# Attention with a gated MLP: the left keys of two heads in one whole product, and the gate's left tokens two blocks at a time

## The chip, the cores and the metric

The kernel runs on one core of one Trainium2 chip. The metric is the device time of the program in microseconds (us), as the median of several runs. The profile shows one execution of it; its span is the time from the first to the last instruction. TensorE is called PE here, VectorE DVE, ScalarE ACT, GpSimd POOL, and SyncE, which issues most transfers, SP.

## What is computed

Eight batches, 12 heads, 448 tokens, 64 features per head. Cut to what matters:

```python
def _attn_ref(q, k, v, g_q, g_k):
    q_n, k_n = (rmsnorm(q, g_q), rmsnorm(k, g_k))
    scores = scale * np.matmul(q_n, k_n.transpose(0, 1, 3, 2))
    scores = scores - np.max(scores, axis=-1, keepdims=True)
    attn = np.exp(scores)
    attn = attn / (np.sum(attn, axis=-1, keepdims=True) + 1e-09)
    return np.matmul(attn, v)

def _moe_ref(x, w_in, g_ln, w_sg, b_sg, w_out):      # x: (8, 448, 768), the heads side by side
    h = gelu_tanh(x @ w_in)                          # 1024 features
    u, v = (h[..., :512], h[..., 512:])
    v_n = layernorm(v) * g_ln
    v_s = np.einsum('ts,bsd->btd', w_sg, v_n) + b_sg[None, :, None]
    return x + (u * v_s) @ w_out
```

448 tokens are three tiles of 128 and one of 64. These last 64 are what the change is about: 64 left keys of each head in attention times v, and 64 left tokens in the gate, the product with w_sg.

## The kernel before

**Precision.** A product of two numbers of full precision is made of three products of halves: each operand is split into a high part and a low part (vh and vl, xh and xl, ws_h and ws_l), and high times high, high times low and low times high are summed in PSUM.

**Pairs and units.** Two heads make a pair, two pairs a unit; there are 48 pairs, six to a batch, and 24 units. A unit's 896 queries are seven tiles of 128. `scores` (L375) makes for each tile the products with the keys (L389) for both heads, the maximum (DVE, L392), the exponentials with their sums (ACT, L394), the high part (ACT, L397) and the low part (DVE, L398), and transposes them by DMA into `at_all` (L403). There a pair has 14 blocks of 128 keys: blocks 0 to 6 of the high parts and 7 to 13 of the low ones. In each seven, blocks 0 to 2 are keys of the first head, 4 to 6 keys of the second, and block 3 has 64 left keys of the first head in its lower partitions and 64 of the second in its upper ones. Two PSUM buffers of two banks each hold the scores (`ps_s`).

**PV.** `load_v` (L286) brings v for three pairs in four transfers, into a tile of seven blocks of 64 columns laid out in the same way. `vsquares` (L343) sums its squares for a scale, `vsplit` (L363) makes vh and vl from it (L369 on ACT, L370 on DVE). `pv` (L431) makes a pair's output in one PSUM bank, the first head in partitions 0 to 63 and the second in 64 to 127. Twelve steps of two matmuls each, one for a head: three steps with the left keys, 64 rows by 64 columns each, and nine with 128 rows by 64 columns. Ahead of them `recips` (L406) makes the row of reciprocals of the sums (POOL, PE at L423, ACT). Behind them the output is scaled and split into xh and xl (L450 to L454).

**The MLP.** `moe` (L477) works on one batch. The v half of h comes first (L510 for the three whole token tiles; L513 for the left 64 tokens, whose two halves of the features stand above each other in a bank), then the u half (L568), with the layer norm in between. Then the gate: for each of four feature blocks f, nine products over whole token tiles and three over the 64 left tokens, which use 64 rows of the array (rows 0 to 63 for f = 0 and 1, rows 64 to 127 for f = 2 and 3, L598); then bias (DVE, L603), the product with u (POOL, L604), the high part (ACT, L605) and the low parts (POOL, L607 and L608). Then the output projection with the residual (L632 to L648). All its PSUM tiles, and a few small ones, share three banks (`ps_m`).

**Order.** The functions are generators. The main loop (from L699) goes over the pairs. In each it merges the steps of three streams by the fraction of them that is done: the scores (8 or 6 steps for a pair), pv of the pair before (4 steps, `SV`) and moe of the batch before (11 steps for most pairs, `MR`). Each `yield` ends a step. The batch's moe starts one pair into the next batch and is spread over some five pairs; for the first and the last batch it starts before its batch is complete (`early`), and the last one has no attention beside it. The Tile framework gives every instruction a number in order of emission; its planner puts the instructions of each engine in order with a simulated timeline, the lowest number first among those that are ready. Instructions of moe go through `low` (L658): it adds an offset (200 or 100) to the number, and after each step sets the number back to what it was:

```python
p = tc.cur_priority
tc.cur_priority = max(1, p + off)
...
next(gen)
...
tc.cur_priority = p
```

So a step of moe does not move the numbers of what is emitted after it. At run time each engine takes its instructions in the planned order.

## Time and profile before

| | |
|---|---|
| median of three runs | 1035.32 us (1034.66 to 1037.95) |
| profiled execution | 1033.44 us |
| its span | 1031.6 us |
| mean granted clock of PE | 0.916 of full speed |
| busy: PE, DVE, ACT, POOL | 829.0, 733.3, 738.1, 386.9 us |
| matmuls | 5844 |

Busy time of PE is the union of its matmuls' times. Matmuls overlap in the pipeline, so what one costs is read from the starts of its neighbours. In a group, `128*64` is the form of the array that a matmul uses: rows by columns. Two matmuls that use different halves of the rows or the columns can run at the same time.

### The profile page before, as it was taken

The page shows a single profiled execution, that of the slowest core. Times are in us where ns is not written, and L with a number is a line of the kernel's source. Part 1 is how long each engine was busy: PE and PEld are TensorE (multiplying, and loading weights), DVE is VectorE, ACT ScalarE, POOL GpSimd, SP SyncE. Part 2 cuts the span into 40 slices and gives each one's busy share as a digit, 9 for nine tenths or more (in the row PEclk, how much of TensorE's full clock was granted, in tenths as well). Part 3 has the DMA queues.
Part 4 walks back from the last instruction along what each step waited for, and adds up shares of the span by engine and source line. Part 5 has one row for each costly group of instructions (what it writes and reads, how often), then busy time and mean ns, then how long its engine had stood idle before and what let it go on. Part 6 is the DMA issues. An engine that isn't in the chain of part 4 may idle for free.

```text
span 1031.6 us, 16639 instructions
## 1 busy us (share of the span) xinstructions
PE 829.0 (80%) x5844; PEld 421.1 (41%) x5844; DVE 733.3 (71%) x1332; ACT 738.1 (72%) x1449; POOL 386.9 (38%) x403
## 2 busy tenths in 40 slices
PE   0243666858798997899689998999779998998798
PEld 0111222324444563346234553446324563454246
DVE  6698888999587667786677758786669666766230
ACT  3767779877868767777768767987777776877351
POOL 1468614567253505243251606341533414030021
PEclk9976687969899999999699998999889999999899
DMA  6998748776886398478886488959967676556102
GB/s 163 214 228 191 166 115 196 185 176 130 181 197 150 88 204 180 98 170 145 186 175 147 99 194 183 182 123 176 194 142 160 141 166 125 106 135 123 40 1 62
DMA packets 448004, 155.70 MB, mean 151 GB/s; under 512 B 404336, under 2 KB 441776, under 8 KB 447920
## 3 DMA queue, kind: packets, MB, share of 16 engines
q1 hardware_dynamic: 447344, 154.18, 69.0%
q8 instruction: 46, 0.75, 0.3%
q10 hardware_dynamic: 576, 0.46, 0.2%
q14 instruction: 38, 0.31, 0.1%
HBM read 43.57 MB, written 11.01 MB: 53 GB/s over the span
## 4 chain that ended last, share of the span: by engine, by line
PE 34%; DVE 21%; ACT 19%; DMA 11%; issue 8%; SPq 4%; POOL 4%; ACTq 0%; POOLq 0%; DVEq 0%
PE pv L446 6%; ACT s L394 5%; DVE ahl L398 5%; PE s L389 4%; DVE nm L392 3%; ACT ahl L397 2%; DMA vr<-in_v_dram 2%; ACT sqk L308 2%; DMA raw<-in_moe_w_in_dram 2%; DMA at<-ahl 2%; POOL qk L330 2%; DMA qt<-hl 2%; DMA qk<-in_k_dram 2%; ACT hl L334 2%; SPq L336 1%
## 5 line engine op out<-in xcount | busy, mean ns | idle before, releaser
L394 ACT ACTIVATE s<-s,nm 128x448 f32<-128x448 f32 x336 | 204.0, 607 | 109.8 <-DVE nm L392 106.8
L398 DVE TENSOR_TENSOR ahl<-s,ahl 128x896 f16<-128x896 f32 x168 | 182.1, 1085 | 100.8 <-ACT ahl L397 99.8
L389 PE MATMUL s<-qt 64*128 64x448 f16 (+1 forms) x1152 | 143.2, 390 | 110.7 <-DVE ahl L398 76.4
L392 DVE TENSOR_REDUCE nm<-s 128x2 f32<-128x896 f32 x168 | 180.8, 1082 | 40.5 <-PE s L389 40.0
L397 ACT ACTIVATE ahl<-s 128x896 f16<-128x896 f32 x168 | 153.4, 920 | 5.3 <-DMA at<-ahl 3.1
L446 PE MATMUL pv<-at,vh 128*64 128x448 f16 (+1 forms) x768 | 122.7, 398 | 16.4 <-DMA at<-ahl 7.6
L413 POOL TENSOR_SCALAR rx<-sums 128x8 f32<-128x8 f32 x48 | 13.4, 278 | 311.8 <-ACT s L394 310.4
L389 PEld LDWEIGHTS <-qt 64*128 64x128 f16 (+1 forms) x1152 | 45.3, 102 | 177.2 <-issue 135.9
L330 POOL TENSOR_TENSOR qk<-qk,ny 128x896 f32<-128x896 f32 x46 | 80.8, 1774 | 85.8 <-DVE ny L125 82.3
L335 POOL TENSOR_TENSOR hl<-qk,hl 128x896 f16<-128x896 f32 x46 | 87.7, 1917 | 55.1 <-ACT hl L334 54.5
L568 PEld LDWEIGHTS <-wi 128*128 128x128 f16 x576 | 55.9, 100 | 60.2 <-issue 14.1
L446 PEld LDWEIGHTS <-vh 128*64 128x64 f16 (+1 forms) x768 | 43.4, 117 | 84.3 <-issue 70.2
L309 DVE TENSOR_REDUCE ss<-sqk 128x14 f32<-128x896 f32 x48 | 51.8, 1080 | 29.2 <-ACT sqk L308 28.9
L394 ACT ACTIVATION_READ_ACCUMULATOR s<-s,nm 128x1 f32 x336 | 67.7, 201 | 0.0
L329 POOL TENSOR_TENSOR qk<-qk,gg 128x896 f32<-128x896 f32 x23 | 48.0, 2085 | 43.2 <-ACT sqk L308 39.3
L423 PE MATMUL row<-ident_h,rh 128*64 128x128 f16 (+1 forms) x384 | 36.7, 240 | 31.7 <-POOL rh L415 24.0
L604 POOL TENSOR_TENSOR gt<-gt,u 128x448 f32<-128x448 f32 x32 | 38.5, 1206 | 60.1 <-DVE gt L603 55.9
L446 PE MATMUL pv<-at,vl 128*64 128x448 f16 (+1 forms) x384 | 60.4, 394 | 0.0
L334 ACT ACTIVATE hl<-qk 128x896 f16<-128x896 f32 x48 | 44.9, 947 | 15.9 <-POOL qk L330 8.4
L308 ACT ACTIVATE sqk<-qk 128x896 f32<-128x896 f32 x48 | 45.6, 951 | 8.2 <-DVE ss L309 4.4
L510 PEld LDWEIGHTS <-xh 128*128 128x128 f16 x288 | 27.0, 101 | 49.2 <-issue 21.9
L369 ACT ACTIVATE vh<-vr,v_s 128x448 f16<-128x448 f32 x48 | 31.9, 668 | 19.7 <-PE pv L446 19.6
(996 smaller groups left out, 1960.8 us busy)
## 6 DMA issues: line engine op xcount, KB each, us to landing
out_dram<-ot SPq DMA_DIRECT2D x56, 192.0 KB, 2.9
vr<-in_v_dram SPq DMA_DIRECT2D x32, 192.0 KB, 3.3
raw<-in_moe_w_in_dram SPq DMA_DIRECT2D x12, 512.0 KB, 5.7
qk<-in_q_dram SPq DMA_DIRECT2D x47, 128.0 KB, 2.8
qk<-in_k_dram SPq DMA_DIRECT2D x47, 128.0 KB, 2.8
vr<-in_v_dram SPq DMA_DIRECT2D x32, 144.0 KB, 3.3
qk<-in_q_dram SPq DMA_DIRECT2D x47, 96.0 KB, 2.6
qk<-in_k_dram SPq DMA_DIRECT2D x47, 96.0 KB, 2.6
```

The source lines that it names most:

```text
L308: A.activation(out=skv, in_=U[u]["qk"][:, x].rearrange("p h c d -> p (h c) d"), func=AF.Square)
L309: V.tensor_reduce(out=SS[u][:, x], in_=skv, axis=AX.X, op=ALU.add)
L330: E.tensor_tensor(out=qk, in0=qk, in1=r["rs"][:, x * SSW:(x + 1) * SSW].unsqueeze(2).broadcast_to([P, SSW, D]), op=ALU.mult)
L334: A.activation(out=h_, in_=r["qk"][:, x], func=AF.Copy)
L335: E.tensor_tensor(out=l_, in0=r["qk"][:, x], in1=h_, op=ALU.subtract)
L389: mm(out=ps[r_, h, 0:S], lhsT=qt[hs, qx, t * P + r_.start:t * P + r_.stop], rhs=qt[hs, kx, j * S:(j + 1) * S], start=(m == 0), stop=(m == 2))
L392: V.tensor_reduce(out=nm, in_=ps[:, :, 0:S], axis=AX.X, op=ALU.max, negate=True)
L394: A.activation(out=ps[:, h, 0:S], in_=ps[:, h, 0:S], func=AF.Exp, bias=nm[:, h:h + 1], accum_out=sums[:, t, h:h + 1])
L397: A.activation(out=ahl[:, 0], in_=ps[:, :, 0:S], func=AF.Copy)
L398: V.tensor_tensor(out=ahl[:, 1], in0=ps[:, :, 0:S], in1=ahl[:, 0], op=ALU.subtract)
L446: mm(out=ps[h * HP:(h + 1) * HP], lhsT=vx[ks, c], rhs=at_all[ks, n + c, o:o + S], start=(k_ == 0), stop=(k_ == len(blocks) - 1), skip_grou ...
L568: done = mm(out=ps[:, 0:S], lhsT=ww[:, g, f * P:(f + 1) * P], rhs=xx, start=(n == 0), stop=(n == 17))
```

## The change

- **v with zeros.** A v tile has eight blocks of 64 columns instead of seven. The left keys of the two heads get a block each, side by side: the first head's stand in the lower partitions of block 3, the second head's in the upper ones of block 4, and the other halves are zero. The tiles are two fixed ones, and POOL writes their zeros once at the start. `vsquares` and `vsplit` go over eight blocks.
- **One product for both heads.** Blocks 3 and 4 of vh or vl are one stationary operand of 128 by 128. The left keys take three whole matmuls instead of six of 64 by 64. The other 18 matmuls stay as they are, but in another order. 24 become 21.
- **A pair's output in one block.** The two yields inside pv go, and one comes after the evacuation; pv has three steps, and `SV` is 3.
- **The left tokens of the v half.** In all batches but the first and the last, moe no longer yields inside the 36 products of the 64 left tokens.
- **The gate two feature blocks at a time.** f = 0 and 2 and then f = 1 and 3: nine whole products of the one, a yield, nine of the other, a yield, then the three products over the left tokens of both in turn, one in rows 0 to 63 and one in rows 64 to 127, each into its own bank. Then the rest for both, and a yield. The gate has six yields instead of eight.

```diff
--- before.py
+++ after.py
@@ -32,7 +32,7 @@
 
 VC, UC = (3,), (0, 1)
 
-SC, SV = 7, 4
+SC, SV = 7, 3
 
 NS, NV, NM = 2, 1, 3
 NQK, NVR, RAWB = 2, 2, 3
@@ -282,6 +282,11 @@
         U[u] = dict(qk=qk)
 
     VR = {}
+    C8 = C7 + 1
+    vr_all = [ld.tile([P, GV, C8, D], F32, name=f"vr{n}", bufs=1) for n in range(NVR)]
+    for x in vr_all:
+        G.memset(x[hi, :, CM], 0.0)
+        G.memset(x[lo, :, C4], 0.0)
 
     def load_v(i):
 
@@ -290,10 +295,10 @@
         if i >= NI:
             return
         b, g = divmod(i, NP)
-        vr = ld.tile([P, GV, C7, D], F32, name="vr", bufs=NVR)
+        vr = vr_all[i // GV % NVR]
         vp = vr.rearrange("p g c d -> p g (c d)")
         src = v[b, 2 * g:2 * (g + GV)].rearrange("(g h) (p c) d -> h p g (c d)", h=2, c=C7)
-        for h, half, s0, c0, n in ((0, lo, 0, 0, C4), (0, hi, 0, C4, CM), (1, lo, C4, C4, CM), (1, hi, CM, 0, C4)):
+        for h, half, s0, c0, n in ((0, lo, 0, 0, C4), (0, hi, 0, C4, CM), (1, lo, C4 + 1, C4, CM), (1, hi, C4, 0, C4)):
             nc.sync.dma_start(out=vp[half, :, s0 * D:(s0 + n) * D], in_=src[h][:, :, c0 * D:(c0 + n) * D])
         for j in range(GV):
             VR[i + j] = vr[:, j].rearrange("p c d -> p (c d)")
@@ -347,7 +352,7 @@
         b, g = divmod(i, NP)
         if g == 0:
             VS["part", b] = sml.tile([P, NP // GV], F32, name="vpart", bufs=2)
-        n = GV * C7 * D
+        n = GV * C8 * D
         sk = prep.tile([P, n], BF16, name="sqv", tag="t4", bufs=HLB)
         x = VR[i]
         A.activation(out=sk, in_=bass.AP(tensor=x.tensor, offset=x.offset, ap=[list(x.ap[0]), [1, n]]), func=AF.Square,
@@ -363,7 +368,7 @@
     def vsplit(i):
         r = R.setdefault(i, {})
         sc = VS[i // NP]["sc"]
-        vh, vl = (att.tile([P, C7, D], F16, name="v" + c, bufs=NVH) for c in "hl")
+        vh, vl = (att.tile([P, C8, D], F16, name="v" + c, bufs=NVH) for c in "hl")
         vr = VR.pop(i)
         vf = vh.rearrange("p c d -> p (c d)")
         A.activation(out=vf, in_=vr, func=AF.Copy, scale=sc)
@@ -432,21 +437,18 @@
         r = R[i]
         vh, vl = r["vh"], r["vl"]
         o = i % NAT * S
-
-        steps = [[(slice(0, P), c + h * C4) if c < CM else (slice(h * HP, (h + 1) * HP), CM) for h in range(2)]
-                 for c in range(C4)]
-        blocks = [(vx, n, hx) for vx, n in ((vh, 0), (vl, 0), (vh, C7)) for hx in steps]
-
-        blocks = blocks[CM::C4] + [x for n, x in enumerate(blocks) if n % C4 != CM]
         row = recips(i)
         yield
         ps = ps_v.tile([P, 512], F32, name="pv")[:, 0:S]
-        for k_, (vx, n, hx) in enumerate(blocks):
-            for h, (ks, c) in enumerate(hx):
-                mm(out=ps[h * HP:(h + 1) * HP], lhsT=vx[ks, c], rhs=at_all[ks, n + c, o:o + S],
-                   start=(k_ == 0), stop=(k_ == len(blocks) - 1), skip_group_check=True)
-            if k_ in (4, 8):
-                yield
+        parts = ((vh, 0), (vl, 0), (vh, C7))
+        for k_, (vx, n) in enumerate(parts):
+            mm(out=ps, lhsT=vx[:, CM:CM + 2].rearrange("p c d -> p (c d)"), rhs=at_all[:, n + CM, o:o + S],
+               start=(k_ == 0), stop=False, skip_group_check=True)
+        for c in range(CM):
+            for vx, n in parts:
+                for h in range(2):
+                    mm(out=ps[h * HP:(h + 1) * HP], lhsT=vx[:, c + h * (C4 + 1)], rhs=at_all[:, n + c + h * C4, o:o + S],
+                       start=False, stop=(c == CM - 1 and n == C7), skip_group_check=True)
         V.tensor_tensor(out=ps, in0=ps, in1=row, op=ALU.mult)
         xh = xp.tile([P, S], F16, name="xh")
         xl = xp.tile([P, S], F16, name="xl")
@@ -454,6 +456,7 @@
         V.tensor_tensor(out=xl, in0=ps, in1=xh, op=ALU.subtract)
         XT[i] = (xh, xl)
         del R[i]
+        yield
 
 
     def cluster(acts, done):
@@ -517,7 +520,7 @@
                 psv[t] = vg[:, tiles[t][1]]
             if early and t == 1 and g == NP - 1:
                 cluster([gelu_v(i) for i in range(2)], done)
-            if st % 2 == 1:
+            if st % 2 == 1 and (early or t != CM or g == NP - 1):
                 yield
         cluster([gelu_v(t) for t in order if not early or t == CM or t > 1], done)
         for t in range(CK):
@@ -578,7 +581,7 @@
                  for f in range(FT)], done)
         yield
         gh = mlp.tile([P, FT, S], F32R, name="gh", tag="vggh")
-        gl = []
+        gl = {}
         vh, vl = V2["vh"], V2["vl"]
         half = slice(b % 2 * HP, (b % 2 + 1) * HP)
         if b % 2 == 0:
@@ -586,26 +589,29 @@
         else:
             gth, gtl, _ = GT[b - 1]
         bb = W["bb"]
-        for f in range(FT):
-            ps = ps_m.tile([P, 512], F32, name="ms_", tag="mm")
-            n = 0
-            for t in range(CK):
-                p0, p1, o = 0, P, t * DH + f * P
-                if t == CM:
-                    p0 = f // 2 * HP
-                    p1, o = p0 + HP, t * DH + f % 2 * P
-                for vx, wx in ((vh, ws_h), (vh, ws_l), (vl, ws_h)):
-                    mm(out=ps[:, 0:S], lhsT=vx[p0:p1, o:o + P], rhs=wx[p0:p1, t], start=(n == 0), stop=(n == 11))
-                    n += 1
-                if t == 1:
-                    yield
-            gt = mlp.tile([P, S], F32, name="gt", tag="gt", bufs=NOT)
-            V.scalar_tensor_tensor(out=gt, in0=ps[:, 0:S], scalar=W["gw"][:, f:f + 1], in1=bb, op0=ALU.mult, op1=ALU.add)
-            G.tensor_tensor(out=gt, in0=gt, in1=u[f], op=ALU.mult)
-            A.activation(out=gh[:, f], in_=gt, func=AF.Copy)
-            gl.append(mlp.tile([P, S], F32R, name="gl", tag="ug", bufs=5))
-            G.tensor_tensor(out=gl[f], in0=gt, in1=gh[:, f].bitcast(F32), op=ALU.subtract)
-            G.tensor_tensor(out=gtl[:, f, half], in0=gt[:, SM:S], in1=gh[:, f, SM:S].bitcast(F32), op=ALU.subtract)
+        for f0 in range(2):
+            psf = {f: ps_m.tile([P, 512], F32, name="ms_", tag="mm") for f in (f0, f0 + 2)}
+            for f, ps in psf.items():
+                n = 0
+                for t in range(CM):
+                    o = t * DH + f * P
+                    for vx, wx in ((vh, ws_h), (vh, ws_l), (vl, ws_h)):
+                        mm(out=ps[:, 0:S], lhsT=vx[:, o:o + P], rhs=wx[:, t], start=(n == 0), stop=False)
+                        n += 1
+                yield
+
+            for n, (vx, wx) in enumerate(((vh, ws_h), (vh, ws_l), (vl, ws_h))):
+                for f, ps in psf.items():
+                    p0, o = f // 2 * HP, CM * DH + f0 * P
+                    mm(out=ps[:, 0:S], lhsT=vx[p0:p0 + HP, o:o + P], rhs=wx[p0:p0 + HP, CM], start=False, stop=(n == 2))
+            for f, ps in psf.items():
+                gt = mlp.tile([P, S], F32, name="gt", tag="gt", bufs=NOT)
+                V.scalar_tensor_tensor(out=gt, in0=ps[:, 0:S], scalar=W["gw"][:, f:f + 1], in1=bb, op0=ALU.mult, op1=ALU.add)
+                G.tensor_tensor(out=gt, in0=gt, in1=u[f], op=ALU.mult)
+                A.activation(out=gh[:, f], in_=gt, func=AF.Copy)
+                gl[f] = mlp.tile([P, S], F32R, name="gl", tag="ug", bufs=5)
+                G.tensor_tensor(out=gl[f], in0=gt, in1=gh[:, f].bitcast(F32), op=ALU.subtract)
+                G.tensor_tensor(out=gtl[:, f, half], in0=gt[:, SM:S], in1=gh[:, f, SM:S].bitcast(F32), op=ALU.subtract)
             yield
         idn = VS[b]["idn"]
         om = [out[x].rearrange("(p c) e -> c p e", c=C7) for x in (b - b % 2, b)]
```

## The prediction

> **What bounds the kernel now.** I read the page's busy shares first, then the busy time by stretches, then the chain that ended last.
>
> ```profile
> PE 829.0 (80%) x5844; PEld 421.1 (41%) x5844; DVE 733.3 (71%) x1332; ACT 738.1 (72%) x1449; POOL 386.9 (38%) x403
> ```
>
> ```profile
> 0.00:227.00 227.00, 110.13 (x690) 46.21 (x691) 190.92 (x343) 162.40 (x316) 112.08 (x98) 0.79 0.79 183
> 227.00:896.00 669.00, 599.22 (x4342) 308.01 (x4341) 489.26 (x905) 506.03 (x1002) 251.41 (x270) 0.95 0.74 156
> ```
>
> ```profile
> PE 34%; DVE 21%; ACT 19%; DMA 11%; issue 8%; SPq 4%; POOL 4%; ACTq 0%; POOLq 0%; DVEq 0%
> PE pv L446 6%; ACT s L394 5%; DVE ahl L398 5%; PE s L389 4%; DVE nm L392 3%; ACT ahl L397 2%; DMA vr<-in_v_dram 2%; ACT sqk L308 2%; DMA raw<-in_moe_w_in_dram 2%; DMA at<-ahl 2%; POOL qk L330 2%; DMA qt<-hl 2%; DMA qk<-in_k_dram 2%; ACT hl L334 2%; SPq L336 1%
> ```
>
> The columns of the second fence are stretch, length, then busy us of PE, PEld, DVE, ACT, POOL, then the granted clock. For the first 227 us DVE is the fullest engine (190.9 of 227). From 227 to 896 us, two thirds of the run, PE is busy 599.2 of 669, that is 0.90, against 0.73 for DVE and 0.76 for ACT. So a microsecond taken off PE in this stretch is worth at most about 0.9, and DVE and ACT have a quarter of their time free to hide a little more work. The chain is shared out, though: PE has only 34% of it, and the products of pv (L446) are its largest line.
>
> **PV: what the zero padding is worth.** The timeline of one pair's output (start, us, matmuls):
>
> ```profile
> 547.71 0.54 PE L568 MATMUL mu__5949<-xh,wi 128*128 128x448 f16 x2
> 548.18 0.38 PE L446 MATMUL pv<-at,vh 64*64 64x448 f16 x2
> 548.39 0.35 PE L446 MATMUL pv<-at,vl 64*64 64x448 f16 x2
> 548.58 1.04 PE L446 MATMUL pv<-at,vh 64*64 64x448 f16 x8
> 549.45 0.73 PE L446 MATMUL pv<-at,vl 128*64 128x448 f16 x6
> 550.02 0.73 PE L446 MATMUL pv<-at,vh 128*64 128x448 f16 x6
> ```
>
> Six 128*64 matmuls start 549.45 to 550.02, 0.57 us: the two heads run side by side, 0.19 us for the two. The two 64*64 matmuls of the left keys also go side by side (548.39 to 548.58, 0.19). So a pair has 12 passes now, and with three whole 128*128 products and nine pairs of column halves it has 12 again. 24 matmuls become 21 and no pass is saved. What can be saved is changes of tile form. A pass of mu takes half of 0.38 us; the two ahead of pv took 0.47 (547.71 to 548.18), so the change of form costs about 0.1 us.
>
> *Entry.* A block that starts in 128*128 form pays none of it where a 128*128 product stands directly ahead. I count 19 of 48 blocks so, the first at 196.39 us, the last here:
>
> ```profile
> 938.58 0.38 PE L510 MATMUL mv__10576<-wi,xl 128*128 128x512 f16 x1
> 938.89 0.38 PE L446 MATMUL pv<-at,vh 64*64 64x448 f16 x2
> ```
>
> No block follows a 64*64 form directly, so nothing is lost: 19 x 0.1 = 1.9 us. The change inside the block stays (64*64 to 128*64 before, 128*128 to 128*64 after).
>
> *One block instead of three.* In 23 of the 48 blocks a score tile (L389) comes in between. The first and the last:
>
> ```profile
> 80.35 0.74 PE L389 MATMUL s<-qt 64*128 64x448 f16 x6
> 81.03 0.38 PE L446 MATMUL pv<-at,vh 128*64 128x448 f16 x1
> ...
> 956.17 0.95 PE L446 MATMUL pv<-at,vh 128*64 128x448 f16 x3
> 957.06 0.74 PE L389 MATMUL s<-qt 64*128 64x448 f16 x6
> 957.73 0.57 PE L446 MATMUL pv<-at,vh 128*64 128x448 f16 x3
> ```
>
> The score tile's three passes take 0.67 (957.06 to 957.73) instead of 0.57, and there is a second change on the way in: 0.2 us for a break, and where it splits the two heads, as behind an odd number (x3, x1), another 0.19. I take 0.28, so 6.4 us in all. With the yields at blocks 4 and 8 gone, the score steps that were emitted between them come behind the whole block. A tile emitted earlier that becomes ready in the middle still breaks in. The bounds are 0 and 6.4; I take two thirds, 4.3, since with the block in the middle of the merge half of the score steps still stand ahead of it.
>
> **Gate: left tokens side by side.** Each batch has 4 feature blocks of 9 whole passes and 3 half-row passes. Emitted as here, six of the latter would run as three twice per batch: 6 x 0.19 = 1.14 us, and 4 of 8 changes of form, 0.4 us: 1.5 us a batch, 12.3 us in all. Whether they are issued so is for the planner, which sorts by a number. `low` puts the number back after each step of moe, so two steps with nothing of the attention emitted between them carry the same numbers and are woven together. The trace shows it, in the last gate and in the left tokens of the v half:
>
> ```profile
> 1000.66 0.36 PE L598 MATMUL ms__11010<-ws_h,vh 64*128 64x448 f16 x1
> 1000.86 0.35 PE L598 MATMUL ms__11010<-ws_l,vh 64*128 64x448 f16 x1
> 1001.14 0.36 PE L598 MATMUL ms__11030<-ws_h,vh 128*128 128x448 f16 x1
> ...
> 1001.91 0.35 PE L598 MATMUL ms__11030<-ws_l,vh 128*128 128x448 f16 x1
> 1002.19 0.36 PE L598 MATMUL ms__11010<-ws_h,vl 64*128 64x448 f16 x1
> 1002.48 0.36 PE L598 MATMUL ms__11030<-ws_h,vl 128*128 128x448 f16 x1
> ```
>
> ```profile
> 518.90 0.30 PE L513 MATMUL mv__5575<-wi,xh 128*64 128x256 f16 x1
> 519.13 0.39 PE L510 MATMUL mv__5655<-wi,xh 128*128 128x512 f16 x1
> 519.45 0.30 PE L513 MATMUL mv__5575<-wi,xh 128*64 128x256 f16 x1
> ```
>
> The gate's leftover block is a step of its own after the steps of f and f+2. After the change v has 10 steps and u 14, so f, f+2 and the leftovers are steps 24 to 26, at 0.227, 0.318 and 0.409 of the batch's third pair (11 steps a pair); the score steps of that pair fall at 0.25 and 0.417. Nothing lies between 0.318 and 0.409: the leftovers of f have numbers among those of f+2's nine products, are ready as soon as f's own nine are done, and go first, alone. The second two fall at 0.5, 0.591 and 0.682, with a score step at 0.583 and none behind it, the same. Then the gate has the 24 passes and 4 changes per two blocks that it has now. I take 2 of the 16 couples as joined (batch 0 has another merge): 1.5 us of the 12.3.
>
> *The v half.* Without its two inner yields the 36 products of the left tokens are one step, but the steps of t = 0 that follow start 9 numbers in, after the first half of one score tile. The weaving of six shown above starts earlier and stays six: 0, between +5 and -5 us (three weavings more or fewer in each of six batches, 0.3 us each: two changes of form and one half-wide pass).
>
> *The end.* The last gate has no scores to fill it. POOL needs three instructions per feature block:
>
> ```profile
> L604 POOL TENSOR_TENSOR gt<-gt,u 128x448 f32<-128x448 f32 x32 | 38.5, 1206 | 60.1 <-DVE gt L603 55.9 <-ACT u L577 2.1 <-ACT s L394 2.0
> L607 POOL TENSOR_TENSOR gl<-gt,gh 128x448 fp32r<-128x448 f32 x32 | 36.8, 1150 | 7.9 <-ACT gh L605 7.8
> L608 POOL TENSOR_TENSOR gtl<-gt,gh 128x64 fp32r<-128x64 f32 x32 | 10.3, 322 | 0.0
> ```
>
> That is 2.7 us a block, more than the 2.3 us of its 12 passes. Two blocks that end together start POOL later and leave it two blocks to finish, and the out projection takes f = 1 second where it now comes third. I charge 0.7 us (0 to 2.7). Elsewhere scores cover this.
>
> **What is added.** The v tile grows from 7 to 8 blocks of 64:
>
> ```profile
> L369 ACT ACTIVATE vh<-vr,v_s 128x448 f16<-128x448 f32 x48 | 31.9, 668 | 19.7 <-PE pv L446 19.6
> L353 ACT ACTIVATE sqv<-vr 128x1344 bf16<-128x1344 f32 x16 | 21.2, 1322 | 10.8 <-DMA vr<-in_v_dram 8.5 <-DVE ss L309 2.3
> L370 DVE SCALAR_TENSOR_TENSOR vl<-vr,v_s,vh 128x448 f16<-128x448 f32 x48 | 36.6, 764 | 3.0 <-ACT vh L369 3.0
> ```
>
> In proportion ACT gets 48 x 0.095 + 16 x 0.189 = 7.6 us and DVE 48 x 0.109 = 5.2 us. Their shares of the chain, 19% and 21%, make 2.5 us of it exposed; the bounds are 0 (the idle quarter hides it) and 12.8. The four memsets on POOL come before its first real work, when it has nothing else, and the v loads move the same bytes through SP: 0.
>
> **Sum.** PE saves 1.9 + 4.3 + 1.5 = 7.7 us, at 0.9 worth 6.9; less 2.5 and 0.7 leaves 3.7. The profiled execution took 1033.44 us (span 1031.6 and 1.84 around it), so 1029.7; the median of the runs is 1.88 above the profiled one, so 1031.6, and I say 1031.5. A difference of 0.3% (3.1 us) is about what can be told from no change.
>
> **Rivals.**
> *The left tokens do go side by side* (chance 0.15). The other 10.8 us x 0.9 = 9.7 come on top: about 1022. For it: couples of row halves do run together in the scores (957.06 above, six in 0.67). Against it: the woven rows.
>
> *No difference* (0.25). PE is 34% of the chain, not 90%: then the 7.7 us are worth 2.6 and the added 2.5 and 0.7 cancel it, about 1036. This also stands for "the change does not do what it says".
>
> *Slower: the unbroken block starves the softmax* (0.22). A score tile that now slips in waits up to the rest of the block, about 1.1 us (half of 12 passes), and with it DVE's maximum, ACT's exponentials and the two score buffers.
>
> ```profile
> PE s L389 <- DVE ahl L398: 76.4, 35, 9.0
> ```
>
> PE already idles 76.4 us ahead of scores for DVE to give a buffer back. In 23 blocks 1.1 us more is 25 us of delay; DVE and ACT hold 40% of the chain, so 10 us, less the 3.7: about 1041.6. It decides from 0.4 us per block on (23 x 0.4 x 0.4 = 3.7).
>
> *Slower by the clock* (0.05). Where PE is starved its granted clock falls: 0.79 in the first 227 us, 0.95 later. If longer waits give two more drops of 6.8 us at half speed, each costs 3.4: 1031.5 + 6.8 = 1038.3. [...]
>
> **Chances and range.** My sum 0.33, the gate 0.15, no difference 0.25, starved 0.22, clock 0.05. Faster 0.48, same 0.25, slower 0.27. Between 1022 and 1042 lie the rivals' times; less than 2 in 10 is outside, in the planner's reordering of everything else. My sum's own range is 1027 to 1032.
>
> **What would show it.** pv in 21 matmuls and about 2.5 us per unbroken block; fewer score tiles inside (8 or so of 48); single 64*128 rows of L598 still 0.19 apart with 128*128 rows between. L369 near 0.76 us, L370 near 0.87. I am wrong if the half-row products come two at a time, if idle time of L389 behind DVE grows past 85 us, or if the clock from 227 to 896 us leaves 0.95.

## The result: slower by 1.4%

The changed kernel took 1050.84 us (median of 4 runs, 1046.84 to 1055.37), the kernel before 1036.3 in the same comparison (1034.66 to 1037.95): a ratio of 1.0142, 95% interval 1.0093 to 1.019. I had said 1031.5, and 1022 to 1042. The profiled execution took 1049.1 us, 15.7 more than the one of before. The head of its page, the first line with the span, the next with each engine's busy time:

```profile
span 1047.3 us, 16365 instructions
...
PE 823.9 (79%) x5700; PEld 420.3 (40%) x5700; DVE 731.5 (70%) x1332; ACT 747.8 (71%) x1449; POOL 385.8 (37%) x407
```

PE is busy 5.1 us less (823.9 for 829.0), in 144 matmuls fewer, and the span is 15.7 us longer. So PE stands idle 223.4 us (1047.3 - 823.9) where it stood idle 202.6 (1031.6 - 829.0). The busy time by stretches (columns as in the prediction) says where:

```profile
0.00:227.00 227.00, 108.75 (x692) 46.08 (x692) 184.31 (x334) 163.21 (x315) 107.83 (x100) 0.80 0.74 175
227.00:896.00 669.00, 579.90 (x4079) 297.83 (x4080) 479.87 (x876) 501.94 (x977) 254.84 (x269) 0.92 0.72 156
```

In the first 227 us PE loses nothing: 692 matmuls for 690, though the kernel now has fewer to do. DVE, the fullest engine there, gets through 334 instructions for 343. Between 227 and 896 us PE is busy 579.9 us for 599.2, its granted clock falls from 0.95 to 0.92, and it gets through 4079 matmuls for 4342; about 93 of these 263 are products that the change merges (144 x 669 / 1032). DVE and ACT do less in the same time as well (876 instructions for 905, 977 for 1002). All three engines wait more. None has become the full one.

The clock has to be taken out of the busy times before they are compared. A block of pv where the clock is low, and two where it is not, from the timeline of the changed kernel (start, us, matmuls):

```profile
563.40 0.35 PE L599 MATMUL ms__6050<-ws_l,vh 128*128 128x448 f16 x1
563.70 0.35 PE L445 MATMUL pv<-at,vh 128*128 128x448 f16 x1
563.89 0.35 PE L445 MATMUL pv<-at,vl 128*128 128x448 f16 x1
564.08 0.35 PE L445 MATMUL pv<-at,vh 128*128 128x448 f16 x1
564.36 0.38 PE L450 MATMUL pv<-at,vh 128*64 128x448 f16 x2
...
566.18 0.36 PE L599 MATMUL ms__6050<-ws_h,vl 128*128 128x448 f16 x1
...
665.03 0.35 PE L571 MATMUL mu__7262<-xh,wi 128*128 128x448 f16 x1
665.22 0.35 PE L445 MATMUL pv<-at,vh 128*128 128x448 f16 x1
...
738.49 0.53 PE L445 MATMUL pv<-at,vh 128*128 128x448 f16 x1 [2.61 <-ACT sqv L358]
738.81 0.58 PE L445 MATMUL pv<-at,vl 128*128 128x448 f16 x1
739.18 0.58 PE L445 MATMUL pv<-at,vh 128*128 128x448 f16 x1
...
743.20 0.59 PE L132 MATMUL psc<-vpart,ones 128*128 128x2 f32 x2
```

The block at 563.70 lasts 2.48 us to the next start; the one at 738.49, behind 2.61 us of idle time, lasts 4.71, with passes 0.37 apart instead of 0.19. The granted clock in the trace is 0.5 or 1 in every record of the two kernels; the block at 738.49 lies in a half-clock stretch of 13.7 us that begins at 730.72, the one at 563.70 at full clock. So I add up the spans by three terms: PE's busy time with the half-clock part counted half ("work"), what the half clock cost, and idle time. Before: 768.8 + 60.2 + 202.6 = 1031.6. After: 753.9 + 70.0 + 223.4 = 1047.3. Work fell by 14.9 us, idle time rose by 20.8, the clock took another 9.8. The work is to be read with care: one of the experiments below changes no matmul and has 9.1 less of it. Busy time counts the modelled end of each run of matmuls, which may be why; that isn't shown.

The places of the idle time, from the groups of the page, first before, then after (behind the bars: busy us and mean ns, then idle time of PE just ahead of the group and its main releasers):

```profile
L389 PE MATMUL s<-qt 64*128 64x448 f16 (+1 forms) x1152 | 143.2, 390 | 110.7 <-DVE ahl L398 76.4
L446 PE MATMUL pv<-at,vh 128*64 128x448 f16 (+1 forms) x768 | 122.7, 398 | 16.4 <-DMA at<-ahl 7.6
```

```profile
L394 PE MATMUL s<-qt 64*128 64x448 f16 (+1 forms) x1152 | 138.6, 381 | 111.6 <-DVE ahl L403 78.2
L445 PE MATMUL pv<-at,vh 128*128 128x448 f16 x96 | 39.0, 406 | 30.1 <-DMA at<-ahl 9.4 <-ACT ahl L402 8.0 <-ACT row L431 7.1
```

Ahead of the scores the sums over the whole span are alike, 110.7 and 111.6, but two changes cancel in them. The wait for DVE alone, between 227 and 896 us, first before, then after (who waits for whom: us in total, times, longest):

```profile
PE s L389 <- DVE ahl L398: 21.0, 21, 3.0
PE s L394 <- DVE ahl L403: 32.5, 22, 4.8
```

In the first 227 us this wait fell from 55.2 to 45.6 us; where the time is lost it rose by 11.5. Ahead of pv PE waits 30.1 us instead of 16.4 over the span. Of these 13.7 us more, 6.9 fall between 227 and 896 us (12.4 for 5.5) and 6.4 in the first 227 us, where PE loses nothing. Ahead of the gate's products it waits 11.2 us in the stretch instead of 0.8, and ahead of the row of reciprocals 10.1 instead of 18.0. So PE's loss is spread over scores, gate and pv.

On the other side of pv stand the engines that evacuate it. Their waits before and after, over the whole span:

```profile
DVE pv L450 <- PE pv L446: 22.0, 11, 7.7
ACT xh L453 <- DVE pv L450: 18.4, 10, 6.2
```

```profile
PE s L394 <- DVE ahl L403: 78.2, 35, 11.0
DVE pv L452 <- PE pv L450: 36.1, 22, 8.5
ACT xh L455 <- DVE pv L452: 25.1, 15, 8.7
DVE nm L397 <- PE s L394: 23.7, 26, 2.2
```

DVE and ACT wait 61.2 us for a pair's output (36.1 + 25.1), before it was 40.4. In three of DVE's waits (up to 416.83, 743.31 and 971.78 us) the next split of a score tile had its input from ACT 0.4 to 0.7 us before the wait ended and ran only behind the scaling of pv; in the others its input came later. Whether PE's longer wait ahead of the scores comes from such waits, no run shows. DVE's own wait for scores fell (23.7; it was 40.0 before).

### The profile page after: what moved, and what is told of

Read it like the earlier page. It is cut to its first block, busy times and chain, and to the rows that moved or that the text cites. A ratio compares the mean times of both kernels' runs of the same rounds, so it can differ in the third digit from the quotient of the medians.

```text
span 1047.3 us, 16365 instructions
## 1 busy us (share of the span) xinstructions
PE 823.9 (79%) x5700; PEld 420.3 (40%) x5700; DVE 731.5 (70%) x1332; ACT 747.8 (71%) x1449; POOL 385.8 (37%) x407
## 4 chain that ended last, share of the span: by engine, by line
PE 35%; ACT 22%; DVE 20%; DMA 9%; issue 7%; POOL 4%; SPq 3%; ACTq 0%; POOLq 0%; DVEq 0%
ACT s L399 7%; PE pv L450 5%; DVE nm L397 5%; ACT ahl L402 4%; DVE ahl L403 4%; PE s L394 3%; DMA vr<-in_v_dram 2%; PE pv L445 2%; DMA raw<-in_moe_w_in_dram 2%; DVE vl L375 2%; DMA at<-ahl 2%; SPq L278 1%; DVE ss L314 1%; ACT sqv L358 1%; ACT vg L499 1%
## 5 line engine op out<-in xcount | busy, mean ns | idle before, releaser
L394 PE MATMUL s<-qt 64*128 64x448 f16 (+1 forms) x1152 | 138.6, 381 | 111.6 <-DVE ahl L403 78.2
L397 DVE TENSOR_REDUCE nm<-s 128x2 f32<-128x896 f32 x168 | 180.5, 1081 | 24.0 <-PE s L394 23.7
L418 POOL TENSOR_SCALAR rx<-sums 128x8 f32<-128x8 f32 x48 | 12.3, 256 | 277.1 <-ACT s L399 275.5
L450 PE MATMUL pv<-at,vh 128*64 128x448 f16 x576 | 102.7, 411 | 0.0
L445 PE MATMUL pv<-at,vh 128*128 128x448 f16 x96 | 39.0, 406 | 30.1 <-DMA at<-ahl 9.4
L450 PE MATMUL pv<-at,vl 128*64 128x448 f16 x288 | 59.3, 409 | 0.0
L374 ACT ACTIVATE vh<-vr,v_s 128x512 f16<-128x512 f32 x48 | 34.4, 721 | 34.3 <-PE pv L450 31.6
L450 PEld LDWEIGHTS <-vh 128*64 128x64 f16 x576 | 36.9, 125 | 48.0 <-issue 34.5
L452 DVE TENSOR_TENSOR pv<-pv,row 128x448 f32<-128x448 f32 x48 | 30.1, 627 | 36.1 <-PE pv L450 36.1
```

The source lines that it names most:

```text
L394: mm(out=ps[r_, h, 0:S], lhsT=qt[hs, qx, t * P + r_.start:t * P + r_.stop], rhs=qt[hs, kx, j * S:(j + 1) * S], start=(m == 0), stop=(m == 2))
L397: V.tensor_reduce(out=nm, in_=ps[:, :, 0:S], axis=AX.X, op=ALU.max, negate=True)
L445: mm(out=ps, lhsT=vx[:, CM:CM + 2].rearrange("p c d -> p (c d)"), rhs=at_all[:, n + CM, o:o + S], start=(k_ == 0), stop=False, skip_group_ ...
L450: mm(out=ps[h * HP:(h + 1) * HP], lhsT=vx[:, c + h * (C4 + 1)], rhs=at_all[:, n + c + h * C4, o:o + S], start=False, stop=(c == CM - 1 and ...
```

## The experiments

Three questions were open: which part of the change costs, whether it costs by its instructions or by the order in which the planner now puts all the others, and whether PE's work is worth anything. The theories are numbered alike in all expectations: 1 the unbroken block of pv, 2 the padded v (its tiles' dependencies or its wider instructions), 3 the gate's two open banks, 4 the order alone, 5 the block in any order, 6 the one step of the v half. All ratios are to the kernel before, run on the same chip, with their 95% intervals.

### One part undone

**Old steps of pv** in the changed kernel (padding, gate and v half kept):

```diff
+                if k_ in (2, 6):
+                    yield
+                k_ += 1
...
         del R[i]
-        yield
```

> The changed kernel with pv's products in three steps again, broken after the same number of passes as before, and SV = 4; the zero-padded v, the gate and the v half stay changed. Theory 1 (the unbroken block is the cost: PE waits for its inputs, 30 us idle ahead of pv instead of 16, and score tiles wait behind it): about 1037 to 1040, ratio to the kernel before 1.00 to 1.005, PE's idle time ahead of pv back to about 16 us. Theory 2 (the wider v tile on ACT and DVE): still 1.012 or more. Theory 3 (the gate's two open banks): still 1.012 or more. Theory 4 (no part costs by itself, the planner lays everything out anew and the order is worse by chance): anything between 0.99 and 1.015.

1.0137 (1.0108 to 1.0166). Undoing the block gives nothing back, where theory 1 allowed 1.005 at most. Its profile has 31.9 us of idle time ahead of pv, so this isn't tied to the block either.

**Old gate** in the changed kernel (diff of the change's gate, reversed):

> The changed kernel with the gate of before, one feature block after the other. Theory 3 (the gate's two open banks and the joint evacuation are the cost): 1.000 to 1.006, PE idle ahead of the gate's products back from 11 us to 1. Theories 1 and 2: still 1.012 or more, since the gate's left tokens ran singly in the changed kernel anyway. Theory 4: anything between 0.99 and 1.015.

1.0114 (1.0092 to 1.0135). Theory 3 allowed 1.006 at most, with PE's wait ahead of the gate back at 1 us; it is still some 8 us.

**Old steps of the v half** in the changed kernel:

```diff
-            if st % 2 == 1 and (early or t != CM or g == NP - 1):
+            if st % 2 == 1:
```

> The changed kernel with the yields inside the left tokens of the v half put back. Theories 1, 2 and 3: 1.010 to 1.016, as the weaving of these products is the same with and without. Theory 4: anything between 0.99 and 1.015.

1.0104 (1.0076 to 1.0132). No part that is taken out brings the kernel back to 1. No single part explains the loss.

### One part alone, on the kernel before

**The v tiles, fixed, and nothing else**, then **the padded v with its 21 products in the old three steps**:

```diff
+    vr_all = [ld.tile([P, GV, C7, D], F32, name=f"vr{n}", bufs=1) for n in range(NVR)]
...
-        vr = ld.tile([P, GV, C7, D], F32, name="vr", bufs=NVR)
+        vr = vr_all[i // GV % NVR]
```

> The kernel before with v loaded into two fixed tiles of seven blocks in turn, as the padded kernel does, instead of tiles from a pool; the same instructions and sizes. Theory 2a (the cost of the padded v is in the tiles: their loads are ordered by other dependencies): 1.008 or more. Theory 2b (it is in the wider instructions on ACT and DVE and in the whole products): within 0.3% of 1.

> The kernel before with the zero-padded v alone: eight blocks, two fixed v tiles, three whole products; pv in its old steps, the gate and the v half as before. It is what the three runs that took one other part back have in common, and each stayed slower by 1.0 to 1.4%. Theory 2 (the padded v is the cost): 1.010 or more, PE idle ahead of pv about 30 us. Theory 1 (the unbroken block): 1.000 to 1.004. Theory 3 (the gate): 1.000 to 1.004. Theory 4 (the order alone): anything between 0.99 and 1.015.

1.0 (0.9986 to 1.0015) and 1.0003 (0.9982 to 1.0024). The page of the second:

```profile
PE 830.8 (80%) x5700; PEld 420.5 (41%) x5700; DVE 733.7 (71%) x1332; ACT 745.0 (72%) x1449; POOL 388.9 (38%) x407
```

The same 5700 matmuls as in the changed kernel and the same wider instructions on ACT and DVE, and no loss and no gain. Theory 2 falls, both halves of it. My charge of 2.5 us for the wider instructions is no more than the upper end of the interval (0.0024), unless savings on PE hide it; and the 144 matmuls fewer are worth nothing that shows, as the prediction had it.

**The block alone** (the old 24 products in one step):

```diff
-SC, SV = 7, 4
+SC, SV = 7, 3
...
-            if k_ in (4, 8):
-                yield
...
         del R[i]
+        yield
```

> The kernel before with pv's 24 products in one step and SV = 3; seven blocks, old gate and v half. Theory 1 (the unbroken block): 1.008 or more, with idle time of PE ahead of pv and of score tiles grown. Theory 2: within 0.4% of 1, or faster by the 4 us of breaks saved.

1.0059 (1.0041 to 1.0078), between theory 1 (1.008 or more) and theory 2 (within 0.4%). PE is busy 815.2 us, 13.8 less than before, and idle 226.1:

```profile
PE s L389 <- DVE ahl L398: 92.2, 37, 8.5
ACT xh L451 <- DVE pv L448: 29.7, 16, 8.8
DVE pv L448 <- PE pv L446: 27.5, 18, 8.5
```

Here PE does wait longer ahead of scores (92.2 for 76.4), as my rival said, and the evacuation of pv too (57.2 for 40.4).

**The gate alone**, and **the v half alone**:

> The kernel before with the gate of the changed one, two feature blocks at a time. Theory 3 (two open banks): 1.005 or more, PE idle ahead of the gate's products about 10 us. Theory 2: within 0.4% of 1, since the left tokens run singly as they do now.

> The kernel before with the 36 left products of the v half in one step, nothing else. It also makes moe two steps shorter, so the order shifts. Theory 6 (the v half's one step is a cost of its own): 1.010 or more. Theory 5 (the block is what costs): 0.996 to 1.006, within the spread that empty steps gave.

1.0112 (1.0096 to 1.0127) and 1.0019 (1.0004 to 1.0033). The second ends theory 6, which asked for 1.010. The first has the ratio that theory 3 asked for without its sign: PE waits some 4 us ahead of the gate there between 227 and 896 us, not 10. The gate alone costs nearly as much as all of the change, yet taking it out of the change gave back little. Costs that don't add up are what an order would make, so the order was tried by itself.

### The order alone

**One empty step** at the head of moe. No instruction of the program is added, taken away or changed; all later steps of moe merge with the attention one place later:

```diff
     def moe(b, done):
...
+        yield
         hs = ...
```

> The kernel before with one empty step at the head of each batch's moe, so that all its later steps merge with the attention one place later (about 1/11 of a pair). Not one instruction is changed. Theory 4 (what costs is the order that the planner lays out, and a tuned order is lost by any shift): 1.004 or more. Theory 3 (the open banks) and theory 1 (the block): within 0.3% of 1.

1.0115 (1.009 to 1.014), 12 us for another order alone. The one instruction more on ACT (1450 for 1449) I took for one more table load, of which the kernel before has 37 at 1.28 us each; no view shows which it is. The page and the stretch from 227 to 896 us show the same signs as in the changed kernel, less of the work, more idle time and a lower clock (759.7 + 72.0 + 214.0 = 1045.7):

```profile
PE 831.7 (80%) x5844; PEld 423.9 (41%) x5844; DVE 740.6 (71%) x1332; ACT 741.1 (71%) x1450; POOL 384.8 (37%) x403
```

```profile
227.00:896.00 669.00, 584.58 (x4249) 302.10 (x4245) 483.49 (x874) 501.27 (x987) 247.52 (x266) 0.93 0.74 154
```

**The gate's yields.** The old gate with two of its inner yields gone, so that it has six steps as the new one has:

```diff
-                if t == 1:
+                if t == 1 and f < 2:
                     yield
```

> The kernel before with the gate's two inner yields of f = 2 and 3 taken out: six steps, as in the changed gate, but one feature block after the other, each in its own bank at its own time. The gate alone cost 1.1%. Theory 3 (two banks held at once and the joint evacuation): within 0.3% of 1. Theory 4 (fewer steps move all later ones, the order is lost): 1.005 or more.

0.9984 (0.9969 to 0.9999). So the number of the gate's steps isn't the cost. PE's order differs from that of the kernel before here too, and theory 4 asked for 1.005 or more: a new order does not always cost.

**The planner's offset** of moe moved from 200 to 210:

> The kernel before with one number of the planner changed: moe's instructions stand 210 behind instead of 200. The same work in a slightly different order. Theory 4 (the order alone moves the time by a per cent): a ratio off 1 by 0.5% or more, either way. Theories 1, 2 and 3: within 0.4% of 1.

1.0006 (0.9991 to 1.0021). This one missed its aim: PE's order came out the same as before's, so it is a second run of the kernel before and says nothing of order.

**Two empty steps before, and one and two in the changed kernel**:

> The kernel before with two empty steps at the head. Theory 4 (its order is one good one among many): 1.003 to 1.015. Theory 5 says nothing of it; if it is within 0.3% of 1, the one-step shift was the odd one, and an order is not lost by any shift.

> The changed kernel with one empty step at the head of each batch's moe: not one instruction changed, the merge one place later. The same edit cost the kernel before 1.15%. Theory 4 (the 1.4% is the loss of a tuned order, the work itself costs nothing): the ratio moves by 0.5% or more from 1.014, and over the two shifts it comes down to 1.006 or less at least once. Theory 5 (pv in one block is slower by itself, whatever the order: the queues of PE, DVE and ACT wait for it): 1.008 to 1.018 in both shifts.

> The changed kernel with two empty steps at the head. Theory 4: 0.99 to 1.018, off the first shift by 0.5% or more. Theory 5: 1.008 to 1.018.

1.0047 (1.0027 to 1.0067) for the kernel before with two; 1.0213 (1.0191 to 1.0236) and 1.0228 (1.0202 to 1.0253) for the changed one. With no, one and two empty steps the kernel before stands at 0, 1.15 and 0.47%, the changed one at 1.42, 2.13 and 2.28%. The spread by order alone is about 1%. The changed kernel is above the kernel before in each place, by 1.0 to 1.8%. It never came down to the 1.006 that theory 4 asked for at least once, and both its shifts lie above the 1.008 to 1.018 of theory 5: neither forecast it.

### PE's work, with the couples made to join

In the changed gate none of the 48 couples of half-row products ran together. One pair of feature blocks, from the timeline:

```profile
676.46 0.35 PE L599 MATMUL ms__7398<-ws_h,vl 128*128 128x448 f16 x1
676.75 0.36 PE L606 MATMUL ms__7398<-ws_h,vh 64*128 64x448 f16 x1
676.95 0.35 PE L606 MATMUL ms__7398<-ws_l,vh 64*128 64x448 f16 x1
677.13 0.35 PE L606 MATMUL ms__7398<-ws_h,vl 64*128 64x448 f16 x1
...
679.73 0.35 PE L599 MATMUL ms__7399<-ws_h,vh 128*128 128x448 f16 x1 [0.25 <-DVE gt L609]
...
681.52 0.36 PE L606 MATMUL ms__7399<-ws_h,vh 64*128 64x448 f16 x1
```

The last of the first block's three half-row products starts 2.6 us before the second block begins. To join them I tied each half-row product behind the last whole product of the second block:

```diff
-  mm(out=ps[:, 0:S], lhsT=vx[:, o:o + P], rhs=wx[:, t], ...)
+  full = mm(out=ps[:, 0:S], lhsT=vx[:, o:o + P], rhs=wx[:, t], ...)
...
-  mm(out=ps[:, 0:S], lhsT=vx[p0:p0 + HP, o:o + P], rhs=wx[p0:p0 + HP, CM], ...)
+  with tc.issue_after(full.ins):
+      mm(out=ps[:, 0:S], lhsT=vx[p0:p0 + HP, o:o + P], rhs=wx[p0:p0 + HP, CM], ...)
```

First on the kernel before with the new gate alone, then on the changed kernel:

> The kernel before with the changed gate, and the half-row products of f tied in issue order behind the last whole product of f + 2, so that they run as couples: 46 of 48 stand next to each other in PE's order, where the gate alone has 3. PE saves 1.1 us a batch in passes and up to 0.4 in changes of form, 12 us in all. If PE's time is what bounds: 0.989 to 0.995 against the kernel before, that is 1.6 to 2.2% less than the gate alone. Theory 3 (two banks held): 1.005 or more, the saving is lost again in waits for banks and for POOL. Theory 4: anything between 0.985 and 1.01.

> The changed kernel with the gate's half-row products tied so that they run as couples (48 of 48 next to each other in PE's order, none in the changed kernel). On the kernel before the tie took 0.9% off the gate alone. Theory 4 with PE's time counting (12 us less on PE): 1.000 to 1.008. Theory 5 (PE is not what bounds while pv stands in one block): 1.010 or more.

1.0025 (1.0008 to 1.0042), with 46 of 48 joined, against 1.0112 untied; and 1.0168 (1.0146 to 1.019) with 48 joined, against 1.0142. In the second, the same two blocks:

```profile
694.85 0.36 PE L607 MATMUL ms__7398<-ws_h,vh 64*128 64x448 f16 x1
694.85 0.36 PE L607 MATMUL ms__7399<-ws_h,vh 64*128 64x448 f16 x1
695.05 0.35 PE L607 MATMUL ms__7398<-ws_l,vh 64*128 64x448 f16 x1
695.05 0.35 PE L607 MATMUL ms__7399<-ws_l,vh 64*128 64x448 f16 x1
695.24 0.35 PE L607 MATMUL ms__7398<-ws_h,vl 64*128 64x448 f16 x1
695.24 0.35 PE L607 MATMUL ms__7399<-ws_h,vl 64*128 64x448 f16 x1
695.52 0.36 PE L599 MATMUL ms__7480<-ws_h,vh 128*128 128x448 f16 x1
```

They share starts, six products in three passes, which by the 0.19 us of a pass saves 0.57 us, twice a batch, as I had worked out. The changed kernel isn't faster for it. Its spans add up as 741.7 + 80.9 + 229.7 = 1052.3: 12.2 us less work than without the ties, 10.9 more at the half clock, 6.3 more idle. The clock from 227 to 896 us:

```profile
227.00:896.00 669.00, 579.20 (x4068) 294.88 (x4069) 481.46 (x874) 497.66 (x972) 255.97 (x270) 0.90 0.73 155
```

On the kernel before, the forecast by PE's time was 0.989 to 0.995, and the ties gave 1.0025. Whether the 0.9% between tied and untied there comes from the passes or from the other order that the ties bring, these runs don't say. A saving of passes alone should have shown in both.

### The parts together

**Padded v with the block**, old gate and old v half:

> The kernel before with the padded v and pv in one block, old gate and old v half: the two pv parts of the change together. Padding alone 0, block alone 0.6%. Theory 5 (the block costs by itself): 1.005 to 1.012. If the parts only add up by way of the order: 0.995 to 1.005. Theory 6: within 0.4% of 1.

1.0194 (1.0179 to 1.0209), though the padding alone gave 1.0003 and the block alone 1.0059. Theory 5 had said 1.005 to 1.012. The same two waits, and PE's ahead of pv:

```profile
DVE pv L452 <- PE pv L450: 38.0, 18, 7.7
ACT xh L455 <- DVE pv L452: 30.3, 19, 8.0
...
PE pv L445 <- DMA at<-ahl: 16.6, 8, 3.8
PE pv L445 <- ACT ahl L402: 11.0, 3, 6.5
```

**The version without the block**: padded v, old steps of pv, old v half, the gate with its couples tied.

> The zero-padded v with pv in its old steps, which alone took as long as the kernel before, and the joined gate (48 of 48 couples next to each other). If PE's time bounds: 0.985 to 0.993. Theory 3: 1.005 or more. Theory 4: anything between 0.985 and 1.01, and not the product of the two parts' ratios.

0.9974 (0.9956 to 0.9992), median 1032.97 us: all couples joined, and a little faster than both kernels, by less than the 0.3% that I called the bound and far from the 0.985 to 0.993 forecast if PE's time bounds. PE waits 26.3 us ahead of pv in it, nearly as long as in the changed kernel, so this wait does not make the loss by itself. Against the changed kernel with the old steps of pv (1.0137) it differs by the ties and the old v half.

All kernels side by side, but for the one with the offset of 210. "Idle" is span less PE's busy time; "pv waits" is DVE's wait for PE's pv plus ACT's for DVE's, as in the waits above; "scores wait" is PE's for DVE ahead of the scores between 227 and 896 us:

| kernel | block | ratio | idle us | pv waits us | scores wait us |
|---|---|---|---|---|---|
| before | no | 1 | 202.6 | 40.4 | 21.0 |
| padded, old steps, gate tied | no | 0.9974 | 210.5 | 42.8 | 21.1 |
| gate's yields | no | 0.9984 | 204.3 | 41.6 | 27.4 |
| fixed tiles | no | 1.0 | 203.6 | 40.0 | 20.2 |
| padded v alone | no | 1.0003 | 201.9 | 36.6 | 20.7 |
| v half alone | no | 1.0019 | 208.6 | 41.4 | 26.7 |
| gate alone, tied | no | 1.0025 | 208.8 | 44.4 | 27.0 |
| before, two empty steps | no | 1.0047 | 218.3 | 51.6 | 37.9 |
| gate alone | no | 1.0112 | 214.3 | 49.0 | 30.4 |
| before, one empty step | no | 1.0115 | 214.0 | 43.6 | 21.4 |
| change, old steps of pv | no | 1.0137 | 237.9 | 43.7 | 32.2 |
| block alone | yes | 1.0059 | 226.1 | 57.2 | 34.5 |
| change, old v half | yes | 1.0104 | 232.6 | 54.4 | 31.3 |
| change, old gate | yes | 1.0114 | 225.4 | 59.4 | 34.8 |
| the change | yes | 1.0142 | 223.4 | 61.2 | 32.5 |
| change, gate tied | yes | 1.0168 | 229.7 | 50.3 | 25.8 |
| padded v and block | yes | 1.0194 | 234.7 | 68.3 | 36.6 |
| change, one empty step | yes | 1.0213 | 230.9 | 60.2 | 32.9 |
| change, two empty steps | yes | 1.0228 | 230.1 | 55.2 | 27.8 |

The ten other kernels without the block average 1.0042, from 0.9974 to 1.0137; the eight with it 1.0153, from 1.0059 to 1.0228. The kernels with the block are thus about 1.1% slower on average, over a scatter (standard deviation) of about 0.6% in either set; the kernels share parts, so this is an average and no interval. The new gate without ties goes with a loss as well, and it is in two of the ten and four of the eight. Without it the averages are 1.0021 (eight kernels) and 1.0134 (four), with it 1.0125 (two) and 1.0172 (four). So each of the two parts goes with about 1% where the other is absent and with about half of that where it is there.

The block goes with pv waits of 50 us and more, where those without it have 37 to 52. That this wait makes the loss is argued, not shown: the slowest kernel without the block has 43.7 us of it and 237.9 us of idle time. The scores wait is 20.2 to 21.1 us in the four kernels at 0.9974, 1, 1.0 and 1.0003, and 25.8 to 37.9 in all others but one; yet the gate's yields have 27.4 at 0.9984 and one empty step 21.4 at 1.0115, so it is no full account either.

## Why the prediction was wrong

- **The step that failed: "a microsecond taken off PE in this stretch is worth at most about 0.9".** I wrote "at most" and then used 0.9 in the sum. A busy share of 0.90 did not make PE the bound here: in this stretch it stood idle 69.8 us before (669 - 599.2), 21.0 of it ahead of the scores for DVE. The changed kernel has up to 14.9 us less work and is 15.7 us longer; with the couples joined it has 27.1 less (768.8 - 741.7) and is 20.7 longer. In these two kernels what was taken off PE came back as idle time and as low clock; in the version without the block, 16.7 us less work (768.8 - 752.1) went with 2.7 us less time (0.26%). My rival "no difference" had the right sentence for this, "PE is 34% of the chain, not 90%", and should have set the exchange rate of the main sum. The rate alone is not the whole miss. At a rate of nothing the sum leaves 1033.44 + 2.5 + 0.7 = 1036.6 us for the profiled execution, which took 1049.1. The other 12.5 us stand for a term that the sum put at nothing: that the waits and the time at the half clock grow. They grew by 20.8 and 9.8 us, against 14.9 us less work.
- **What I left out of the sum: the order.** I put the planner's reordering into the 2 in 10 outside. One empty step costs 1.15%, over three times the gain I forecast (3.7 of 1033.44 us, 0.36%). The change moves steps in four places, so a sum of parts could not be trusted to less than this scatter.
- **Entry and breaks of pv** (1.9 + 4.3 us on PE): the mechanism came true and more. No block has a score tile inside, where I had expected some 8, and the block above takes 2.48 us, 2.5 forecast. A block starts 0.19 behind a 128*128 product in one row (665.03) and 0.30 in another (563.40), so the 0.1 us isn't always saved. By the work figure, with the scatter of some 9 us that it has, PE gained what I counted, and the time did not.
- **The gate** (1.5 us for 2 of 16 couples): right that the planner would not put the halves side by side, by the reason given; it was none instead of two (the 16 couples of feature blocks are the 48 couples of products above). The price of the joined case, 12.3 us on PE for all couples, agrees with the 12.2 us less work in the changed kernel, as far as that figure goes; that the rest of it would be worth 9.7 us of time was not so.
- **What is added.** L374 takes 721 ns and L375 883, forecast 760 and 870:

```profile
L374 ACT ACTIVATE vh<-vr,v_s 128x512 f16<-128x512 f32 x48 | 34.4, 721 | 34.3 <-PE pv L450 31.6 <-DVE v_s L141 2.6
L375 DVE SCALAR_TENSOR_TENSOR vl<-vr,v_s,vh 128x512 f16<-128x512 f32 x48 | 42.3, 883 | 2.0 <-ACT vh L374 0.8
```

  The durations were about right. Of the 2.5 us of time nothing shows: the padding alone costs 0.0003 (0.9982 to 1.0024).
- **The end** (0.7 us): nothing. From the last gate's first POOL instruction to its last it takes 12.04 us after, as before:

```profile
1013.02 1.13 POOL L610 TENSOR_TENSOR gt<-gt,u 128x448 f32<-128x448 f32 x1 [35.92 <-DVE gt L609]
...
1024.73 0.33 POOL L614 TENSOR_TENSOR gtl<-gt,gh 128x64 fp32r<-128x64 f32 x1
```

- **The v half** (0, between +5 and -5): 1.0019, 2 us, inside the bounds.
- **The rivals.** "The unbroken block starves the softmax" was the nearest: right sign, 1041.6 for it, 1041.6 us measured for the block alone. The agreement to the digit is chance. In the block alone PE does idle more ahead of scores (92.2 us). In the whole change the sum stays under the mark of 85 that I named (78.2), but a mark over the whole span was the wrong one: between 227 and 896 us the wait rose from 21.0 to 32.5 us. The unbroken block isn't shown to be what starves the softmax, since the change with the old steps of pv has 32.2 us of it there. The clock rival came true in part: the clock left 0.95 for 0.92 between 227 and 896 us, and over the span the half clock cost 9.8 us more, against 6.8 forecast (two stretches of 6.8 us; 8 of the 22 at half clock before have that length). Its condition, longer waits, was not met by the longest of them: PE's longest idle time in this stretch is 5.27 us before and 4.83 after, while the half clock begins 10 times there before and 15 times after. In the 10 us ahead of each of the 15 the longest idle time is between 0.98 us (ahead of 450.82) and 3.82 us (ahead of 228.96), and PE is idle for 16 to 46% of the 10 us. So short waits went with the half clock too.
- **What stays open.** What makes the loss beyond the rate. The block and the untied gate each go with a part of it, but why, and why the change without the block is slow too (1.0137), isn't shown. No run held the order of everything else fixed while pv alone was changed; that was not tried.

## What to carry to other kernels

Where a planner mixes several streams, take the worth of an engine's time from its share of the chain and its idle time, not from how busy it is: here 14.9 us less work of PE went with 20.8 us more of its idle time. Read waits in the stretch where the time is lost, since over the whole span a rise and a fall can cancel. Before any part of such a change is judged, shift the schedule by an empty step or two in both kernels; here that alone gave 1%, more than the effect sought. A long block without breaks, alone, went with less busy time of PE here (815.2 us for 829.0) and with longer waits of the engines that empty it (57.2 us for 40.4). Try the parts of such a change one by one, and together, since their costs did not add.

## What the hardware showed

Two 64*64 products of opposite corners of the array already shared a pass in the kernel before (0.19 us for the two, from 548.39 to 548.58), and merging them into a 128*128 product with zeros saved no time: 1.0003 (0.9982 to 1.0024) with 144 matmuls fewer. Half-row products of two blocks shared starts where they stood next to each other in PE's order (two at 694.85 us with the ties, which put all 48 couples so), and none of the 48 couples did in the changed kernel. The lost clock is a large term: the half clock cost 60.2 us before, 70.0 after and 80.9 with the couples joined. It need not be less work that lowers it, since one empty step, with the same matmuls as before, lost 72.0.
